# Threshold attention and SwiGLU block on one core: weight clamps of the first tiles on GpSimd, one weight conversion in another slot, one flipped head copied earlier

## The chip, the core and the metric

The kernel runs on one core of one Trainium2 chip. The metric is the device time of one execution in microseconds (us), given as the median of several runs. The engines named below are TensorE (PE; its weight loads PEld), VectorE (DVE), ScalarE (ACT), GpSimd (POOL) and SyncE (SP), which only issues DMAs here. Each engine works through its own queue in order; semaphores hold an instruction back until what it reads is there and what it overwrites has been read.

## What is computed

All inputs are float32.

```python
# q, k, v: (8, 8, 576, 64); tau = 0.02
scores = scale * np.matmul(q, k.transpose(0, 1, 3, 2))
thresh = np.max(scores, axis=-1, keepdims=True) - tau
scores = np.where(scores >= thresh, scores, -1000000000.0)
attn = softmax(scores)
attn_out = np.matmul(attn, v)
# x: (4608, 512), the heads side by side
g = x @ w_gate                      # w_gate, w_val: (512, 1536)
out = (g * sigmoid(g)) * (x @ w_val) @ w_out    # w_out: (1536, 512)
```

## The kernel before

**Float64 weights as two words.** The three weight matrices reach the chip as 64-bit words, two 32-bit words for each weight, and each piece of 128 x 768 weights is made into float32 by integer and float steps, a "conversion". There are 24 pieces. `fetch_weights` (L268) issues a piece's DMAs on SP into one of six places, if the piece's place is free. `split_weights` (L286) issues two ScalarE instructions: L291 makes the upper part (and writes it where the weight will lie), L292 the lower part (into one of three rotating buffers). `join_weights` (L295) does the rest: on DVE a clamp with a minimum and a maximum (L298, `tensor_scalar` with two operations), a shift by three bits (L302) and a `scalar_tensor_tensor` that puts in the sign (L305), then on GpSimd the integer addition of the lower part (L307). The clamp needs L291 alone, the addition needs L305 and L292. A place is free for the next piece when the piece before has been joined.

**The first batch.** The first of the eight batches is worked on in a loop that is written out by hand (L665): four segments of two tiles (each segment one pair of heads, tiles t = 0 and 1 of 128 queries), then four segments of three tiles (t = 2, 3 and the half tile t = 4, for the pairs 3, 0, 1, 2). A slot "n.x" is tile x of segment n: 0.0, 0.1, 1.0, ... 3.1 are the first pass, 4.0, 4.1, 4.2, 5.0, ... 7.2 the second. The pieces of one slot come in this order:

- `scores` (L398) is a generator in four steps. First: the score matmuls on PE (L407, or L413 for the half tile) into one or two of the two score buffers in PSUM, and the negated maximum of each head on DVE (L424). Second: ScalarE's threshold (L427) and exponential (L428) of each head. Third: DVE's mask with sum (L431) for each head, the sum (L433) and its reciprocal (L434); from t = 2 on also the scaling of the probabilities by it, head 0 on ScalarE (L441), head 1 on GpSimd (L439). Fourth: for t = 0 and 1 two scaled unit matrices instead (L447).
- `attend_tile` (L487): the attention product of the tile flipped before (PE, L500 and L503), copied by ScalarE (L505).
- `flip` (L454): the transposes of the probabilities of the tile before. For each head four PE instructions into a bank "tp" (L469 or L471), more into a bank "end" (L474, L476, L480); ScalarE copies each head's bank (L477, L481) and then the end bank (L483). Four PSUM banks go round in turn among these, the attention products and the gate and value products; a bank is given back after its copy has been queued, and the next user's matmul waits for that copy.
- `split_weights` and `fetch_weights(2)`, then step three of the scores, then `join_weights` of one piece, then `fill` (PE's gate and value products of the first block, L517, with ScalarE's L532 and L533, DVE's L541), step four, and `fill` again. GpSimd's gate product (L548) comes from `gates`.
- At the slot's end, in some slots: DVE's transposes of the next segment's k and q (L628, L631, L635, L705, L639, L640) and GpSimd's scaling of q (L340).

In the second step of a slot ScalarE's queue so holds: threshold and exponential of both heads, then the copies of both flipped heads and of the end, then L291 and L292, then the scaling.

**Where a slot differs.** In 4.0 the kernel before attends twice, and joins, splits and fetches a second piece after the products. In 4.2 and 5.2 (`double`) it joins two pieces, after the products rather than before, and splits and fetches a second one.

**After the first batch** a planner (`Plan`, L28) orders the instructions of the other engines around PE's by costs written in the source. Its remaining conversions are lines L820 to L834. The first slot after the loop (scores L1652) is called H0.

Of the kernel before, what the change touches and what calls it, by code (L numbers as in the profile page):

```python
# [14 lines left out]
ALU = mybir.AluOpType  # L15
# [97 lines left out]
def kernel(  # L113
# [11 lines left out]
    nc = tc.nc  # L125
    P = 128
    B, H, S, D = q.shape
    NP = H // 2
# [10 lines left out]
    NT = SM // P  # L139
# [87 lines left out]
    def bank(name):  # L227
        n = turns.popleft()
        ps = ps_f.tile([P, 512], F32, name=name, tag=f"bank{n}")
        taken[id(ps)] = n, ps  # L230
        return ps

    def give_back(ps):
        turns.append(taken.pop(id(ps))[0])

    def run_idle(n):
        ps = bank("idle")
        for _ in range(n):
            nc.tensor.matmul(ps[:, 0:TC], ones[:, 0:P], ones, start=True, stop=True)
        give_back(ps)  # L240
# [27 lines left out]
    def fetch_weights(n=1):  # L268
        for _ in range(n):
            if not wpieces or wpieces[0][2] in used:  # L270
                return
            dst, srcs, place = wpieces.popleft()
            used.add(place)
            m = 2 if len(srcs) == 2 else nf
            to = places[place].bitcast(U64).rearrange("p (m n) -> p m n", m=m)
            if len(srcs) == 1:
                nc.sync.dma_start(out=to, in_=srcs[0])
            else:
                for x, src in enumerate(srcs):
                    nc.sync.dma_start(out=to[:, x, :], in_=src)  # L280
            fetched.append((dst, place))

    def words(place, dst, w):
        return places[place].bitcast(U32).rearrange("p (m n w) -> p m n w", m=dst.shape[1], w=2)[:, :, :, w]

    def split_weights():  # L286
        if fetched:
            dst, place = fetched.popleft()
            lo = los[0].rearrange("p (m n) -> p m n", m=dst.shape[1])
            los.rotate(1)  # L290
            nc.scalar.activation(dst, words(place, dst, 1).bitcast(F32), AF.Abs, scale=2.0 ** -96)  # L291
            nc.scalar.activation(lo, words(place, dst, 0), AF.Identity, bias=minus2, scale=-2.0 ** -51)  # L292
            split.append((dst, place, lo))

    def join_weights(n=1):  # L295
        steps = [split.popleft() for _ in range(min(n, len(split)))]
        for up, place, lo in steps:
            nc.vector.tensor_scalar(out=up, in0=up, scalar1=1.875 * 2.0 ** -80, scalar2=2.0 ** -111,  # L298
                                    op0=ALU.min, op1=ALU.max)
        for up, place, lo in steps:  # L300
            ub = up.bitcast(U32)
            nc.vector.tensor_scalar(out=ub, in0=ub, scalar1=3, scalar2=None, op0=ALU.logical_shift_left)  # L302
        for up, place, lo in steps:
            ub = up.bitcast(U32)
            nc.vector.scalar_tensor_tensor(out=ub, in0=words(place, up, 1), scalar=0x80000000, in1=ub,  # L305
                                           op0=ALU.bitwise_and, op1=ALU.bitwise_xor)
            nc.gpsimd.tensor_tensor(out=ub, in0=ub, in1=lo.bitcast(U32), op=ALU.add)  # L307
            joined.append(up)
            used.discard(place)
# [82 lines left out]
    def turned(t):  # L392
        return TA <= t < NT
# [58 lines left out]
    xts = {}  # L452

    def flip():  # L454
        if not unflipped:
            return
        seg, t, both, ps = unflipped.popleft()
        n = P if t < NT else D
        pT = pTbufs[0][:, 0:2 * KT * n].rearrange("p (h t q) -> p h t q", h=2, t=KT)
        pT2 = pTbufs[0][:, 2 * KT * n:(2 * KT + 1) * n]  # L460
        pTbufs.rotate(1)
        end = bank("end")
        for h, (p, unit) in enumerate(ps):
            tp = bank("tp")
            for kt in range(KT):
                at_ = kt * P + (D if turned(t) and h == 1 else 0)
                ks, to = slice(at_, at_ + P), slice(kt * P, (kt + 1) * P)
                if unit is ident:
                    nc.tensor.transpose(tp[:, to], p[:, ks], unit)  # L469
                else:  # L470
                    nc.tensor.matmul(tp[:, to], p[:, ks], unit, start=True, stop=True)  # L471
            if t < NT:
                if not turned(t):
                    nc.tensor.matmul(end[h * D:(h + 1) * D, 0:P], p[:, KM:S], unit, start=True, stop=True)  # L474
                elif h == 1:
                    nc.tensor.transpose(end[:, 0:P], both, unit)  # L476
                nc.scalar.copy(pT[:, h], tp.rearrange("p (t q) -> p t q", q=P))  # L477
            else:
                for hs in heads:
                    nc.tensor.matmul(end[hs, 0:D], p[hs, KM:S], unit[hs, hs], start=True, stop=True)  # L480
                nc.scalar.copy(pT, tp.rearrange("p (t h q) -> p h t q", h=2, q=D))  # L481
            give_back(tp)
        nc.scalar.copy(pT2, end[:, 0:n])  # L483
        give_back(end)
        unattended.append((seg, t, pT, pT2))

    def attend_tile():  # L487
        if not unattended:
            return
        if not xts:  # L490
            for u, lo in enumerate((0, 2 * XW)):
                xts["full", u] = xall[:, lo:lo + XW].rearrange("p (c n) -> p c n", c=NCC)
            xts["last", 0] = xlast
        seg, t, pT, pT2 = unattended.popleft()
        vr, vr2 = seg["v"]
        n = pT2.shape[1]
        xa = bank("xa")
        for kt in range(KT):
            for h in range(2):
                nc.tensor.matmul(xa[h * D:(h + 1) * D, 0:n], vr[:, h, kt, :], pT[:, h, kt, :],  # L500
                                 start=(kt == 0), stop=False)
        for hs in heads:
            nc.tensor.matmul(xa[hs, 0:n], vr2[hs, :], pT2[hs, :], start=False, stop=True)  # L503
        u, lo = divmod(t * P, TC)
        nc.scalar.copy(xts[("last", 0) if t == NT else ("full", u)][:, seg["i"], lo:lo + n], xa[:, 0:n])  # L505
        give_back(xa)
# [136 lines left out]
    def give(unit):  # L643
        ready.append(unit)
        left[0] += cost(unit)
# [17 lines left out]
    more_loads.popleft()()  # L663
    last = iter(())
    for n, seg in enumerate(segs[:2 * NP]):  # L665
        if n >= NP:
            seg["v"] = segs[seg["i"]]["v"]
        for x, t in enumerate(seg["tiles"]):
            go = scores(seg, t)
            next(go)  # L670
            if not n and not x:
                run_idle(6)
            next(last, None)
            attend_tile()
            next(go)
            next(last, None)
            flip()
            if n == NP and x == 0:
                attend_tile()
                give(FIRST)  # L680
            part = pace(n, x) / 2
            more = len(split)
            if n or x:
                split_weights()
                fetch_weights(2)
            next(go)
            double = t == NT and NP <= n < NP + 2
            if more and not double:
                join_weights()
            fill(part)  # L690
            next(go)
            fill(part)
            if double:
                join_weights(2)
                split_weights()
                fetch_weights(2)
            elif n == NP and x == 0:
                join_weights()
                split_weights()
                fetch_weights(2)  # L700
            gates()
            last = go
            if n == NP and later:
                to, fr = later.pop(0)
                nc.vector.transpose(out=to, in_=fr)  # L705
            if x == 0 and 0 < n < NP - 1:
                load_v(segs[n + 1])
                more_loads.popleft()()
            if n == 0 and x == 1 or n == 1:
                scales.popleft()()  # L710
            elif n == NP - 2 and x == 1:
                more_loads.popleft()()
                scales.popleft()()
            elif n == NP - 1:
                scales.popleft()()
                fetch_qk(NP)
            elif n == NP and x == 1:
                scales.popleft()()
            if x == len(seg["tiles"]) - 2 and n + 1 < len(segs):
                prepare(segs[n + 1])  # L720
# [1180 lines left out]
    for s, (n, x) in enumerate((n, x) for n in range(len(halved)) for x in range(NU3)):  # L1901
        seg = halved[n]
        i, t = seg["i"], seg["tiles"][x]
# [104 lines left out]
```

## Time and profile before

| what | us |
|---|---|
| median of three runs | 1380.66 |
| lowest, highest | 1379.52, 1382.99 |
| the profiled execution: its time | 1379.44 |
| the profiled execution: its span | 1377.3 |
| mean granted TensorE clock | 1.0 of full speed |

The span runs from the first to the last instruction that the profile records; 2.1 us of the profiled execution's time lie around it.

Where PE starts the scores of each slot in the profiled execution (us from the span's start):

| slot | start | slot | start | slot | start |
|---|---|---|---|---|---|
| 1.0 | 16.36 | 4.0 | 53.63 | 6.0 | 98.93 |
| 1.1 | 22.54 | 4.1 | 64.09 | 6.1 | 105.97 |
| 2.0 | 28.59 | 4.2 | 71.22 | 6.2 | 114.89 |
| 2.1 | 34.84 | 5.0 | 77.10 | 7.0 | 120.76 |
| 3.0 | 41.66 | 5.1 | 84.54 | 7.1 | 126.65 |
| 3.1 | 47.90 | 5.2 | 93.07 | 7.2 | 133.64 |
| | | | | H0 | 139.50 |

How to read the profile's lines. A group or timeline line names the line of the kernel, the engine, the operation, what is written and what is read, with partitions x elements. A timeline line begins with the start and the duration; in brackets stands how long the engine had been idle before and what ended that. A line of the waits names the engine and its line, then what it waited for, then the total, the number of times and the longest. A line of the windows gives the stretch, its length, the busy time of PE, PEld, DVE, ACT and POOL with the number of instructions, the granted clock, the DMA share and GB/s. In the page's slices each digit is a fortieth of the span and the busy share in tenths.

### The profile page before, as it was taken

How to read it: one execution, taken by the hardware profiler on the slowest of the kernel's cores; microseconds unless marked ns; L12 is line 12 of the kernel's file. 1: busy time of each engine (PE TensorE's matmuls, PEld its weight loads, DVE VectorE, ACT ScalarE, POOL GpSimd, SP SyncE). 2: the span in 40 equal slices, each digit the busy share in tenths (PEclk: the TensorE clock that was granted, in tenths of full speed). 3: DMA queues.
4: the chain of work that ended last, by engine and by line, in shares of the span. 5: the costliest groups of instructions: out<-in, count | busy, mean ns of one | idle time of the engine just before them, and what ended most of it. 6: DMA issues, size and time to landing. Idle time of an engine off the chain costs nothing.

```text
span 1377.3 us, 39288 instructions
## 1 busy us (share of the span) xinstructions
PE 1356.8 (99%) x15630; PEld 1116.4 (81%) x15630; DVE 1081.5 (79%) x2829; ACT 875.1 (64%) x2278; POOL 700.2 (51%) x649
## 2 busy tenths in 40 slices
PE   9988999999999999999999999999999999999998
PEld 6666787778778778887788888878887888999998
DVE  7988988887887777787678877877777776687786
ACT  6888766676755767767766766776677764330330
POOL 2456498844484669533974378436943593000000
PEclk9999999999999999999999999999999999999999
DMA  8734413465513541555155523553065404423421
GB/s 176 208 105 142 99 36 98 122 188 143 174 48 126 143 115 42 170 143 143 32 153 133 146 56 121 139 143 96 27 186 157 112 19 143 158 80 138 154 69 32
DMA packets 208295, 162.33 MB, mean 118 GB/s; under 512 B 166128, under 2 KB 180464, under 8 KB 202736
## 3 DMA queue, kind: packets, MB, share of 16 engines
q1 hardware_dynamic: 203920, 158.86, 40.9%
q8 instruction: 124, 2.03, 0.6%
q10 hardware_dynamic: 4192, 0.95, 0.3%
q14 instruction: 59, 0.48, 0.1%
HBM read 138.28 MB, written 21.50 MB: 116 GB/s over the span
## 4 chain that ended last, share of the span: by engine, by line
PE 91%; DVE 4%; ACT 2%; SPq 1%; DMA 1%; issue 1%; ACTq 0%; DVEq 0%
PE pb L940 18%; PE pa L940 12%; PE px L1420 12%; PE sc L1652 10%; PE xa L1749 9%; PE pe L940 9%; PE po L1216 5%; PE py L1429 5%; PE sc L1101 2%; PE pg L1147 2%; PE pv L1147 2%; PE pv L517 1%; PE pe L1101 1%; SPq L336 1%; PE xa L500 1%
## 5 line engine op out<-in xcount | busy, mean ns | idle before, releaser
L1700 DVE SCALAR_TENSOR_TENSOR pall<-sc,th,pall 128x288 f32<-128x288 f32 x504 | 243.7, 514 | 63.5 <-ACT pall L1698 49.3
L940 PE MATMUL pb<-xall,big 128*128 128x256 f32 x1152 | 273.5, 380 | 0.0
L1698 ACT ACTIVATE pall<-sc,nm 128x288 f32<-128x288 f32 x504 | 231.6, 497 | 34.6 <-DVE pall L1700 34.3
L940 PEld LDWEIGHTS pb<-xall,big 128*128 128x128 f32 x1152 | 216.4, 190 | 31.0 <-issue 2.2
L1728 DVE STREAM_TRANSPOSE pall<-pall 128x576 f32<-128x576 f32 x252 | 190.0, 765 | 59.3 <-ACT pall L1726 42.6
L1726 ACT ACTIVATE pall<-pall,ri 128x288 f32<-128x288 f32 x408 | 186.6, 527 | 25.0 <-DVE ri L1714 24.3
L795 POOL TENSOR_TENSOR hall<-hall,tmp 128x512 f32<-128x512 f32 x80 | 103.6, 1295 | 159.3 <-DVE hall L993 144.0
L940 PE MATMUL pa<-xall,big 128*128 128x256 f32 x768 | 183.3, 382 | 0.0
L940 PEld LDWEIGHTS pa<-xall,big 128*128 128x128 f32 x768 | 143.1, 190 | 22.0 <-issue 2.9
L1652 PE MATMUL sc<-kT,qT 64*32 64x144 f32 (+1 forms) x5376 | 149.8, 345 | 3.4 <-DVE pall L1700 2.2
L1673 DVE TENSOR_REDUCE mx<-sc 128x2 f32<-128x576 f32 x168 | 124.7, 742 | 27.3 <-PE sc L1652 26.9
L1652 PEld LDWEIGHTS sc<-kT,qT 64*32 64x32 f32 x5376 | 97.9, 106 | 57.5 <-issue 21.6
L940 PE MATMUL pe<-xall,big 128*128 128x256 f32 x576 | 137.3, 381 | 0.0
L1749 PE MATMUL xa<-pall,vall 64*32 64x288 f32 x4032 | 132.2, 404 | 1.0 <-DVE hall L993 0.8
L1723 POOL TENSOR_SCALAR pall<-pall,ri 128x288 f32<-128x288 f32 x96 | 95.7, 1010 | 63.6 <-DVE ri L1714 63.5
L940 PEld LDWEIGHTS pe<-xall,big 128*128 128x128 f32 x576 | 108.4, 190 | 17.0 <-issue 2.7
L1749 PEld LDWEIGHTS xa<-pall,vall 64*32 64x32 f32 x4032 | 76.4, 107 | 50.1 <-issue 7.2
L1708 ACT COPY sums<-sums 32x6 f32<-32x6 f32 x336 | 66.6, 198 | 45.1 <-DVE pall L1700 40.5
L1687 ACT COPY mx<-mx 32x6 f32<-32x6 f32 x196 | 38.1, 194 | 60.8 <-DVE mx L1675 58.9
L992 ACT ACTIVATE vall<-tmp 128x512 f32<-128x512 f32 x96 | 60.1, 629 | 23.9 <-POOL tmp L795 9.6
L1429 PE MATMUL py<-wo,hall 128*128 128x256 f32 x336 | 74.8, 379 | 0.0
L1675 DVE TENSOR_REDUCE mx<-sc 128x1 f32<-128x288 f32 x168 | 74.7, 444 | 0.0
(256 smaller groups left out, 2468.2 us busy)
## 6 DMA issues: line engine op xcount, KB each, us to landing
big<-sums_hbm SPq DMA_DIRECT2D x42, 1024.0 KB, 5.3
big<-sums_hbm SPq DMA_DIRECT2D x48, 768.0 KB, 4.8
vall<-in_v_dram SPq DMA_DIRECT2D x112, 144.0 KB, 3.1
out_dram<-big SPq DMA_DIRECT2D x32, 256.0 KB, 3.5
qT<-in_q_dram SPq DMA_DIRECT2D x112, 72.0 KB, 4.8
kT<-in_k_dram SPq DMA_DIRECT2D x112, 72.0 KB, 3.1
wo<-in_moe_w_gate_dram SPq DMA_DIRECT2D x16, 384.0 KB, 3.8
wo<-in_moe_w_val_dram SPq DMA_DIRECT2D x16, 384.0 KB, 4.5
```

What stands on the lines that cost most here:

```text
L795: return lambda: nc.gpsimd.tensor_tensor(out=out, in0=a, in1=b, op=op)
L940: nc.tensor.matmul(ps[:, i], w[:, k_, i * P:(i + 1) * P], x[:, k_, :], start=first and i == k_ == 0, stop=True, skip_group_check=True)
L1420: nc.tensor.matmul(ps, a[:, f, :], ws[n][:, f, :], start=bank_ not in begun, stop=True, skip_group_check=True)
L1429: nc.tensor.matmul(ps(), a[:, f, i * P:(i + 1) * P], operands[o][:, f, :], start=first and f == 0, stop=True, skip_group_check=True)
L1652: nc.tensor.matmul(pss[h][(slice(g * G, (g + 1) * G), *part)], qT[hs, col:col + G], kT[hs, c * SH + keys[0]:c * SH + keys[1]], start=True, ...
L1673: rs.append(job("DVE", 0.72, lambda n=n, tile_=tile_: nc.vector.tensor_reduce(out=mx[:, n:n + 2, 0], in_=tile_[:, :, 0:SH], axis=AX.X, op= ...
L1698: ej = job("ACT", 0.42, lambda x=x, n=n: nc.scalar.activation(ps[x], scs[x], AF.Exp, bias=nm[:, n:n + 1]), ej, *((masks[h, 0], masks[h, 1] ...
L1700: masks[x] = job("DVE", 0.45, lambda x=x, n=n: nc.vector.scalar_tensor_tensor(out=ps[x], in0=scs[x], scalar=th[:, n:n + 1], in1=ps[x], op0 ...
L1723: scaled.append(job("POOL", 1.02, lambda x=x, n=n: nc.gpsimd.tensor_scalar(out=x, in0=x, scalar1=ri[:, n:n + 1], scalar2=None, op0=ALU.mul ...
L1726: scaled.append(job("ACT", 0.46, lambda x=x, n=n: nc.scalar.activation(x, x, AF.Copy, scale=ri[:, n:n + 1]), rj, rank=rank))
L1728: seg["turned"].append(job("DVE", 0.72, lambda both=both: nc.vector.transpose(out=both, in_=both), *scaled, rank=rank))
L1749: nc.tensor.matmul(holds[a].ap()[x * G:(x + 1) * G, 0:SH].rearrange("d (i q) -> d i q", q=G), vr[rs, h, j, ds], p[rs, h, :, j, :], start=( ...
```

## The change

Three things, all in the first batch.

1. In segments 0 to 3 the clamp is issued to GpSimd right after a piece's two ScalarE instructions, in the slot that splits it; `join_weights` leaves the clamp out for such a piece. Seven pieces are split there (slots 0.1 to 3.1). The clamp's place in GpSimd's queue is ahead of the addition of the piece joined in the same slot and of the scaling of q at the slot's end.
2. The second join, split and fetch of slot 4.0 are gone; slot 6.2 is now a `double` slot like 4.2 and 5.2. Every conversion between the two is joined one piece later in the sequence; from 7.0 on the slots hold the same pieces as before.
3. `flip` becomes a generator, and in the second tile of segments 4 to 7 (slots 4.1, 5.1, 6.1 and 7.1) its first head is issued before the second step of the scores. On ScalarE one head's copy (L477) so stands ahead of both thresholds and exponentials instead of behind them.

The order of PE's and SP's instructions is the same in both kernels.

```diff
--- before.py
+++ after.py
@@ -283,6 +283,11 @@
     def words(place, dst, w):
         return places[place].bitcast(U32).rearrange("p (m n w) -> p m n w", m=dst.shape[1], w=2)[:, :, :, w]
 
+    early_slots, clamped = [True], []
+
+    def clamp(eng, x):
+        eng.tensor_scalar(out=x, in0=x, scalar1=1.875 * 2.0 ** -80, scalar2=2.0 ** -111, op0=ALU.min, op1=ALU.max)
+
     def split_weights():
         if fetched:
             dst, place = fetched.popleft()
@@ -290,13 +295,16 @@
             los.rotate(1)
             nc.scalar.activation(dst, words(place, dst, 1).bitcast(F32), AF.Abs, scale=2.0 ** -96)
             nc.scalar.activation(lo, words(place, dst, 0), AF.Identity, bias=minus2, scale=-2.0 ** -51)
+            if early_slots[0]:
+                clamp(nc.gpsimd, dst)
+                clamped.append(dst)
             split.append((dst, place, lo))
 
     def join_weights(n=1):
         steps = [split.popleft() for _ in range(min(n, len(split)))]
         for up, place, lo in steps:
-            nc.vector.tensor_scalar(out=up, in0=up, scalar1=1.875 * 2.0 ** -80, scalar2=2.0 ** -111,
-                                    op0=ALU.min, op1=ALU.max)
+            if not any(up is x for x in clamped):
+                clamp(nc.vector, up)
         for up, place, lo in steps:
             ub = up.bitcast(U32)
             nc.vector.tensor_scalar(out=ub, in0=ub, scalar1=3, scalar2=None, op0=ALU.logical_shift_left)
@@ -452,6 +460,10 @@
     xts = {}
 
     def flip():
+        for _ in flip_steps():
+            pass
+
+    def flip_steps():
         if not unflipped:
             return
         seg, t, both, ps = unflipped.popleft()
@@ -480,6 +492,7 @@
                     nc.tensor.matmul(end[hs, 0:D], p[hs, KM:S], unit[hs, hs], start=True, stop=True)
                 nc.scalar.copy(pT, tp.rearrange("p (t h q) -> p h t q", h=2, q=D))
             give_back(tp)
+            yield
         nc.scalar.copy(pT2, end[:, 0:n])
         give_back(end)
         unattended.append((seg, t, pT, pT2))
@@ -663,6 +676,7 @@
     more_loads.popleft()()
     last = iter(())
     for n, seg in enumerate(segs[:2 * NP]):
+        early_slots[0] = n < NP
         if n >= NP:
             seg["v"] = segs[seg["i"]]["v"]
         for x, t in enumerate(seg["tiles"]):
@@ -672,9 +686,13 @@
                 run_idle(6)
             next(last, None)
             attend_tile()
+            flips = flip_steps()
+            if n >= NP and x == 1:
+                next(flips, None)
             next(go)
             next(last, None)
-            flip()
+            for _ in flips:
+                pass
             if n == NP and x == 0:
                 attend_tile()
                 give(FIRST)
@@ -684,7 +702,7 @@
                 split_weights()
                 fetch_weights(2)
             next(go)
-            double = t == NT and NP <= n < NP + 2
+            double = t == NT and NP <= n < NP + 3
             if more and not double:
                 join_weights()
             fill(part)
@@ -692,10 +710,6 @@
             fill(part)
             if double:
                 join_weights(2)
-                split_weights()
-                fetch_weights(2)
-            elif n == NP and x == 0:
-                join_weights()
                 split_weights()
                 fetch_weights(2)
             gates()
```

## Prediction

> **What bounds the kernel now.** I read the page first, then the windows, the waits of the first 140 us, and each engine's timeline there. A slot n.x is tile x of segment n in the loop at L665; "H0" is the first slot after that loop. The page's head:
>
> ```profile
> span 1377.3 us, 39288 instructions
> PE 1356.8 (99%) x15630; PEld 1116.4 (81%) x15630; DVE 1081.5 (79%) x2829; ACT 875.1 (64%) x2278; POOL 700.2 (51%) x649
> ```
>
> TensorE sets the end: it is free for 20 us of the whole span. Windows cut at the score starts of 1.0, 4.0, 5.0, 6.0, 7.0 and H0 (us, then busy time by engine):
>
> ```profile
> 53.63:77.10 23.47, 20.90 (x159) 15.71 (x158) 20.20 (x39) 19.96 (x40) 13.77 (x8) 1.00 0.58 172
> 77.10:98.93 21.83, 18.98 (x148) 13.99 (x147) 18.44 (x35) 17.60 (x35) 12.96 (x7) 1.00 0.33 110
> ...
> sum 123.14, PE 112.70 PEld 84.14 DVE 106.82 ACT 103.39 POOL 64.27; mean PE 22.54 PEld 16.83 DVE 21.36 ACT 20.68 POOL 12.85
> ```
>
> Half of that, 10.4 us, is PE's idle time in the first batch, 16.36 to 139.50, where the change acts; besides this only scores that stretch because their second half waits (2.02 us below, else 1.36) can be shortened. DVE is busy 107 of 123 us, hence nearly as tight. The waits of the first 140 us (total, times, longest):
>
> ```profile
> PE pv L517 <- ACT big L477: 6.4, 4, 2.3
> ...
> PE sc L407 <- DVE pall L431: 2.9, 4, 1.0
> ```
>
> In four slots a value product waits for ScalarE's copy of a flipped head (its bank); in four more the scores wait until DVE has masked the tile before. Rows that I price with (start, duration), from the timelines of PE, DVE and GpSimd (POOL):
>
> ```profile
> 28.59 2.02 PE L407 MATMUL sc<-pall,qT 64*128 64x288 f32 x8 [0.41 <-DVE pall L431]
> ...
> 69.73 1.56 PE L517 MATMUL pv<-xall,big 128*128 128x256 f32 x6 [2.28 <-ACT big L477]
> ```
>
> ```profile
> 29.57 0.76 DVE L298 TENSOR_SCALAR big<-big 128x768 f32<-128x768 f32 x1
> 30.36 0.56 DVE L302 TENSOR_SCALAR big<-big 128x768 uint32<-128x768 uint32 x1
> ...
> 60.41 0.98 DVE L302 TENSOR_SCALAR big<-big 128x768 uint32<-128x768 uint32 x1
> ...
> 62.55 2.23 DVE L298 TENSOR_SCALAR big<-big 128x768 f32<-128x768 f32 x1 [0.16 <-ACT big L291]
> ```
>
> ```profile
> 28.99 0.92 POOL L340 TENSOR_SCALAR hall<-hall,scl 128x256 f32<-128x256 f32 x1 [2.06 <-DMA hall<-in_q_dram]
> ...
> 60.09 1.88 POOL L439 TENSOR_SCALAR pall<-pall,ri 128x576 f32<-128x576 f32 x1 [0.84 <-DVE ri L434]
> 62.53 1.83 POOL L307 TENSOR_TENSOR big<-big,extra 128x768 uint32<-128x768 uint32 x1 [0.57 <-ACT big L291]
> ...
> 74.87 1.72 POOL L340 TENSOR_SCALAR qT<-qT,scl 128x576 f32<-128x576 f32 x1
> ```
>
> A clamp (L298) is usually 0.54 us, but stretches until a running GpSimd instruction is over; a shift (L302) beside one took 0.98 instead of 0.56.
>
> [...] L340 takes 0.92 us for 256 elements and 1.72 for 576, 2.5 ns each. [...]
>
> **The change, part by part.** I carried the four queues forward slot by slot with the rows' durations, in each engine's new order; PE and SP keep their order.
>
> *A. Seven clamps leave DVE (conversions split in slots 0.1 to 3.1).* Each took 0.57 us, start to start, between a tile's masks and the next tile's maxima. PE alone needs 5.73 us for such a slot (3.1: 47.90 to 53.63, no wait). Score starts 22.54, 28.59, 34.84, 41.66, 47.90, 53.63 make slots of 6.05, 6.25, 6.82, 6.24, 5.73: 2.44 us over the floor, the most that A can bring by 4.0. GpSimd gains seven clamps. No row shows a two-operation one; the L340 line gives 2.2 us for 768 elements with one operation, the 768-element L307 1.8, and twice 2.2, the second operation paid like the first, 4.4. I take 2.5 and keep 1.8 to 4.4. GpSimd's slot is then 2.5 + 1.81 (add) + 1.08 (scaling of 320 elements of q, L340) = 5.4, under 5.73, and a clamp has until the next slot's shift: hidden. Behind the clamp wait the add and q's scaling, which slide later by 2.5, so that two or three shifts (L302) now meet a scaling of q and lose 0.2 to 0.9 each, as the clamp at 29.57 did. Some 0.4 of the 2.44 is given back: -2.0 at 4.0. In 4.0 the exponentials and copies that the second attention product waits for come 0.6 earlier (the last clamp): -2.6 at 4.1. Neither end helps by itself, since nothing else on GpSimd gets shorter; the low end costs nothing, because GpSimd stands idle 2.2 to 6.3 us ahead of each add in the first pass (25.13 to 56.38).
>
> *B. The conversion moved out of 4.0.* DVE's 3.73 us from 62.55 to 66.28 go (the clamp 2.23, because of L307). The maxima of 4.1 (66.71) can follow the scores, at about 64.85. ScalarE loses 1.7 us (L291, L292), SP a pair of weight loads that nobody waits for. The later W_out conversion waits 0.79 for its DMA today; splitting it a slot later ends that, off the path.
>
> *C. The head copied first in 4.1, 5.1, 6.1, 7.1.* The copy (0.47) goes ahead of the exponentials and waits for PE's transposes; behind it in ScalarE's queue stand both exponentials, and DVE's masks wait for these. In 4.1: transposes end about 65.9, copy to 66.45, exponentials to 68.1, first mask 68.1. PE goes on with pv at 67.35 rather than 69.73 and starts the scores of 4.2 at 68.7 rather than 71.22. B and C: -2.5, so -5.1 at 4.2. Slot 4.2 gives back 0.8, since its transposes wait for probabilities scaled as late as before: -4.3 at 5.0. In 5.1 and 6.1 the copy fits into ScalarE's idle time before L427 (1.50, 1.40), and 1.70 and 1.64 us of PE's wait go. But the next maxima still wait behind DVE's conversion (94.75) and then behind ScalarE's queue, which is shorter only by the one copy: I keep 0.47 each, -5.2 at 7.0.
>
> *D. The conversion arrives in 6.2.* DVE then has two there, 3.8 us before 7.0's maxima, as 5.0 and 6.0 have: those slots took 7.44 and 7.04 against 5.89 of 7.0: 1.35 more on average. With half of the 0.78 by which the scores that follow stretch (2.14 for 1.36), +1.7. In 7.1 the removed 0.80 wait pays 0.3 of it. In 7.2 DVE, now behind, has two transposes of q and k in its queue as well (L639, L640: 1.4 us), and H0's scores wait for its masks: +1.4. Together +2.8.
>
> Sum: -5.2 + 2.8 = -2.4 us at H0 (139.5). From there on each queue's order is the old one, so the shift is carried to the end. The profiled execution took 1379.44 (span 1377.3 and 2.1 around it): 1377.0. The median of the three runs is 1.2 higher: 1380.66 - 2.4 = **1378.3**.
>
> **Rivals.** *GpSimd becomes the bound (17%).* From the first split part (18.0) to the scaled head that 4.1's transposes need, GpSimd must do 7 clamps, 6 adds (10.9), the scalings of q (6.2) and L439 (1.9): 37.0 + 7c, against 63.3 in my account. It decides from c = 3.8, eats the whole gain at 4.1, and at c = 4.4 ends 7 x 0.64 = 4.5 later: **1382.8, slower than before**. For it: one-input rows are far from cheap, and two operations may cost double. Against: the add of two inputs with 768 elements is 1.8.
>
> *DVE swallows it (15%).* After a double conversion two adds and a gate run on GpSimd, and L298 grew to 1.08 and 1.49 us (85.52, 106.94) in 5.0 and 6.0. If 7.0 and H0 catch the same, 0.95 each, the gain is 0.5: 1380.2.
>
> *PE keeps what C frees (8%).* If DVE catches up in 5.2 and 6.2, the 3.3 us of waits there are kept rather than 0.94: 1375.9. Against it: DVE runs at 18.4 of 21.8 us there and has its maxima last.
>
> That the change doesn't do what it says is out: the built order has each move.
>
> **Numbers.** My forecast 60%, 1.2 us either way. Range 1375.8 to 1382.8: it leaves out the clamps beyond 4.4 and half of the third rival, under 2 in 10. A measurement of this kernel tells about 0.3% (4.1 us) from no change: faster (under 1376.5) 8%, slower (over 1384.8) 10%, between 82%.
>
> **What would show it.** Right: GpSimd's new clamps between 1.8 and 3.5 us; scores at about 51.6 (4.0), 66.1 (4.2), 72.8 (5.0), 115.6 (7.0), 137.1 (H0), so a lead that peaks near 5 us and halves in 7.x; the pv wait for L477 gone in four slots. Wrong: L439 of 4.0 starting after 61; exponentials of 4.1 ending after 67; a lead at 7.0 under 3 or at H0 over 4; or shifts in the first pass of more than 1.5 us.

## The result, and the profile after

| | before | after |
|---|---|---|
| median, us (18 executions each) | 1380.06 | 1377.72 |
| lowest, highest | 1377.64, 1382.99 | 1376.52, 1380.42 |
| the profiled execution: time, span | 1379.44, 1377.3 | 1378.87, 1376.8 |
| mean granted TensorE clock in it | 1.000 | 0.998 |

The ratio of the two is 0.9985, with a 95% interval of 0.9978 to 0.9992: 1.1 to 3.0 us less. The forecast was 2.4 us less, the medians differ by 2.3.

The head of the page after the change:

```profile
span 1376.8 us, 39287 instructions
PE 1358.2 (99%) x15630; PEld 1119.1 (81%) x15630; DVE 1076.9 (78%) x2822; ACT 874.5 (64%) x2278; POOL 709.1 (52%) x656
```

DVE has lost 4.6 us and GpSimd gained 8.9; PE is 1.4 us busier with the same 15630 instructions. Why it is so shows in the windows, cut at the same score starts as before:

```profile
52.16:74.06 21.90, 20.41 (x160) 15.57 (x159) 15.28 (x32) 17.61 (x37) 12.93 (x8) 1.00 0.55 159
74.06:95.35 21.29, 18.75 (x147) 14.08 (x146) 18.45 (x35) 17.98 (x36) 12.99 (x8) 1.00 0.44 151
...
116.64:139.76 23.12, 21.65 (x147) 16.47 (x146) 19.39 (x37) 17.04 (x35) 13.00 (x7) 0.85 0.25 76
```

Segment 4 (first line) takes 21.90 us instead of 23.47, with DVE busy 15.28 instead of 20.20. The last line is segment 7: its granted clock, the third number from the end, is 0.85. Before, it was 1.00 in each of these segments. Finer windows of PE alone (stretch, length, busy time, clock, DMA share, GB/s) find the place:

```profile
123.00:124.00 1.00, 0.00 (x0) 1.00 1.00 387
124.00:125.00 1.00, 0.93 (x5) 1.00 0.78 301
125.00:126.00 1.00, 1.00 (x7) 0.68 0.00 0
126.00:127.00 1.00, 1.00 (x6) 0.50 0.00 0
...
131.00:132.00 1.00, 1.00 (x4) 0.50 0.00 0
132.00:133.00 1.00, 1.00 (x6) 0.90 0.00 0
```

PE stands still from 122.6 to 124.07, goes on, and 1.3 us later gets half the clock for 6.8 us (a window that holds a change has a value between the two: 0.68 puts it at 125.36, 0.90 at 132.20). The PE timeline of the changed kernel shows what was waited for, and what half the clock costs:

```profile
65.64 1.46 PE L530 MATMUL pv<-xall,big 128*128 128x256 f32 x6
67.02 1.19 PE L421 MATMUL sc<-pall 64*64 64x288 f32 x8
...
70.76 1.09 PE L481 MATMUL tp<-pall 128*128 128x128 f32 x8 [1.16 <-ACT tmp L546]
...
74.06 1.36 PE L415 MATMUL sc<-pall 64*128 64x288 f32 x10
...
124.07 2.82 PE L415 MATMUL sc<-pall 64*128 64x288 f32 x10 [1.47 <-DVE pall L439]
...
128.28 1.97 PE L481 MATMUL tp<-pall 128*128 128x128 f32 x8
```

The first value product of 4.1 (65.64) no longer waits, and 4.2 starts 4.20 us earlier than before. Eight transposes take 1.97 us at 128.28 and 1.09 at 70.76. If PE does half its work in these 6.8 us, as the granted clock says, it loses 3.4 us there: an estimate. The waits of the first 140 us (16 to 140; total, times, longest):

```profile
PE tp L481 <- ACT tmp L546: 3.9, 3, 1.4
...
PE sc L415 <- DVE pall L439: 3.6, 4, 1.5
```

The wait of pv for the copy of a flipped head (6.4 us before) is gone. In its place, the transposes of the third slot of a segment wait 3.9 us for a bank: it held the gate product of the slot before until ScalarE's L545 and L546 had read it, and these stand behind the split (L296, L297) and the scaling (L449).

The clamps on GpSimd, with a scaling of q beside them:

```profile
18.10 0.83 POOL L289 TENSOR_SCALAR big<-big 128x768 f32<-128x768 f32 x1 [6.97 <-ACT big L296]
18.90 0.93 POOL L348 TENSOR_SCALAR extra<-extra,scl 128x256 f32<-128x256 f32 x1
...
42.20 1.34 POOL L289 TENSOR_SCALAR big<-big 128x768 f32<-128x768 f32 x1 [3.40 <-ACT big L296]
```

A clamp of 768 elements takes 0.83 us, 1.1 ns per element, less than L348 with 256.

### The profile page after: what moved, and what is told of

Read it like the earlier page. It is cut to its first block, busy times and chain, and to the rows that moved or that the text cites. A ratio compares the mean times of both kernels' runs of the same rounds, so it can differ in the third digit from the quotient of the medians.

```text
span 1376.8 us, 39287 instructions
## 1 busy us (share of the span) xinstructions
PE 1358.2 (99%) x15630; PEld 1119.1 (81%) x15630; DVE 1076.9 (78%) x2822; ACT 874.5 (64%) x2278; POOL 709.1 (52%) x656
## 4 chain that ended last, share of the span: by engine, by line
PE 93%; DVE 4%; ACT 2%; issue 1%; DMA 0%; DVEq 0%; ACTq 0%
PE pb L954 18%; PE pa L954 12%; PE px L1434 12%; PE sc L1666 10%; PE xa L1763 9%; PE pe L954 9%; PE po L1230 5%; PE py L1443 5%; PE sc L1115 2%; PE pg L1161 2%; PE pv L1161 2%; PE sc L415 1%; PE pe L1115 1%; PE tp L483 1%; PE xa L513 1%
```

## The experiments

A lead is the start of a slot's scores in the profile before, less that in the profile shown, each counted from the start of 1.0. "Next" is the scores after H0 (150.49 before).

| lead, us | 4.0 | 4.1 | 4.2 | 5.0 | 5.2 | 6.0 | 7.0 | 7.1 | 7.2 | H0 | next |
|---|---|---|---|---|---|---|---|---|---|---|---|
| forecast | 2.0 | 2.6 | 5.1 | 4.3 | | | 5.2 | 3.5 | | 2.4 | 2.4 |
| after | 1.46 | 1.64 | 4.19 | 3.03 | 4.95 | 3.57 | 4.11 | 2.57 | -0.27 | -0.27 | -0.27 |
| e9_fill_ahead | 1.71 | 1.90 | 4.44 | 3.30 | 5.22 | 3.85 | 4.37 | 2.93 | 2.81 | 1.83 | 1.53 |
| e1_clamps | 1.48 | 1.67 | 2.30 | 2.32 | 2.33 | 2.33 | 2.34 | 2.34 | 2.34 | 2.34 | 2.34 |
| e2_flips | 0.06 | 0.07 | 1.99 | 0.65 | 2.57 | 1.19 | 1.74 | 1.74 | 2.80 | 2.12 | 1.81 |
| e3_move | 0.06 | 0.06 | 1.37 | 1.39 | 1.39 | 1.39 | 1.39 | -0.15 | -1.71 | -1.71 | -1.71 |
| e4_no_move | 1.45 | 1.63 | 4.17 | 2.79 | 4.71 | 3.34 | 3.90 | 3.91 | 4.97 | 4.25 | 3.97 |

Every execution lists its mean clock. One stretch of 3.4 us at half clock takes 0.0012 from it, so 0.999 can hide one such stretch (the profiled executions of e1, e3 and e6 have one each; e1's lies at 8 us, ahead of 1.0, where eight score matmuls took 1.99 us, 1.25 in the changed kernel), and a low clock in the last microseconds counts too (0.50 from 1376.5 on in the profile before). The last column compares only those at 1.000, with those of the kernel before in the same comparison (for "after", whose comparison lists none for before, with those of e1's: 1378.71).

| | median, us | ratio to before, 95% interval | executions at 0.998 or less, at 0.999 | at 1.000, less before at 1.000 |
|---|---|---|---|---|
| before (with e1 to e4) | 1379.52 | | 13, 10 of 33 | |
| after | 1377.72 | 0.9978 to 0.9992 | 6, 5 of 18 | -1.7 |
| e1_clamps | 1376.50 | 0.9967 to 0.9986 | 0, 3 of 10 | -2.2 |
| e2_flips | 1377.10 | 0.9975 to 0.9990 | 1, 2 of 16 | -1.8 |
| e3_move | 1381.05 | 1.0001 to 1.0018 | 6, 4 of 13 | +1.9 |
| e4_no_move | 1374.77 | 0.9951 to 0.9976 | 0, 1 of 5 | -4.1 |
| e5_fill | 1379.85 | 0.9994 to 1.0011 | 7, 1 of 13 | -0.3 |
| e6_two_clamps | 1378.65 | 0.9982 to 0.9999 | 7, 4 of 13 | -1.5 |
| e7_all_clamps | 1379.79 | 0.9989 to 1.0005 | 11, 2 of 13 | none |
| e8_flips_x12 | 1375.13 | 0.9959 to 0.9982 | 0, 2 of 6 | -3.5 |
| e9_fill_ahead | 1377.30 | 0.9975 to 0.9989 | 0, 2 of 21 | -1.5 |
| e10_late_split | 1378.60 | 0.9986 to 0.9999 | 14, 6 of 21 | -1.8 |
| e11_no_move_fill | 1374.33 | 0.9948 to 0.9973 | 0, 1 of 5 | -4.4 |
| e12_before_fill | 1380.03 | 0.9993 to 1.0010 | 4, 4 of 13 | -0.4 |

The two tables fit: the lead at "next" is what the executions at full clock gain (e1 2.34 and 2.2, e2 1.81 and 1.8, e3 -1.71 and -1.9, e4 3.97 and 4.1, e9 1.53 and 1.5). The before's own 13 executions at 0.998 or less have a median of 1380.81, 2.1 us over its 10 at 1.000. So two things set a median here: the work in the first batch, and how often the clock drops.

### The parts by themselves

**e1_clamps**: the changed kernel without its second and third part.

```diff
-            if n >= NP and x == 1:
+            if False:
                 next(flips, None)
...
-            double = t == NT and NP <= n < NP + 3
+            double = t == NT and NP <= n < NP + 2
...
+            elif n == NP and x == 0:
+                join_weights()
+                split_weights()
+                fetch_weights(2)
```

> The clamps alone on GpSimd in the first pass; the conversion stays in 4.0 and the flips stay behind the exponentials. If the parts add as the prediction has them (part A): the scores of 4.0 start about 1.5 us earlier, as in the changed kernel (52.2), the lead is carried to H0, and the time is 1.5 to 1.9 us under before. If the first pass's gain is lost again as soon as DVE is the busiest engine (rival): the lead is under 0.5 us at 5.0 and the time within 0.5 us of before. The granted clock is 1.00 throughout in either case.

Measured: 1.48 at 4.0 as expected, then 0.63 more in 4.1, 2.34 at H0, 3.0 us less in the median. More than either theory had. The 0.63 come where pv waits in 4.1 (start, duration, and the wait that was 2.28 before):

```profile
68.34 1.56 PE L530 MATMUL pv<-xall,big 128*128 128x256 f32 x6 [1.64 <-ACT big L489]
```

**e2_flips**: the third part alone (the clamp on DVE, the conversion in 4.0).

```diff
-            if early_slots[0]:
+            if False:
                 clamp(nc.gpsimd, dst)
```

with e1's last two hunks.

> The flipped head copied first in 4.1, 5.1, 6.1 and 7.1 alone; clamps on DVE, the conversion in 4.0. Prediction's part C: four waits of PE for the head's copy go (6.4 us in all), of which 1 to 2 us are kept at H0, since DVE's maxima and masks come last in the next slot: 1.0 to 1.8 us under before. Rival (PE keeps what the copy frees): 3 us or more under before. Other rival (the new wait of the flipped transposes for the tanh's bank, 3.9 us in three slots of the changed kernel, takes its place): within 0.5 us of before.

Measured: 1.81 at "next", 2.4 less in the median (1.8 at full clock); both rivals fall. Its PE timeline in 4.1 and 4.2:

```profile
69.38 1.19 PE L421 MATMUL sc<-pall 64*64 64x288 f32 x8 [0.54 <-DVE pall L439]
...
73.31 1.09 PE L481 MATMUL tp<-pall 128*128 128x128 f32 x8 [1.36 <-ACT tmp L546]
```

Of 1.92 us gained in 4.1 the second line takes back 1.34 in 4.2 (lead 0.65 at 5.0): the new wait belongs to the flips, not to the clamps or the move.

**e3_move**: the second part alone (e1's first hunk and e2's hunk in the changed kernel).

> The conversion alone moved from 4.0 to 6.2. Prediction's parts B and D: about 1.2 us gained at 4.1, some 2.8 us given back between 7.0 and H0: 0.8 to 1.6 us over before, with the clock at 1.00. Clock theory: PE waits for DVE in 7.0 and 7.1 about 1.4 us at a time, the granted clock halves for some 7 us around 125 to 135 us in part of the executions (mean clock 0.997 to 0.999 rather than 1.000), and the time is 1.5 to 4 us over before, more in the executions with the lower clock.

Measured: 1.5 us over before in the median, and 3.1 us lost in segment 7, where PE waits twice:

```profile
126.92 2.13 PE L415 MATMUL sc<-pall 64*128 64x288 f32 x10 [1.46 <-DVE pall L439]
...
133.98 1.56 PE L530 MATMUL pv<-xall,big 128*128 128x256 f32 x6 [1.27 <-ACT big L489]
```

Both theories get their part. The queues alone cost the forecast's amount, at a clock of 1.00 in this stretch; and 6 of 13 executions have the lower clock. In the profiled one it fell elsewhere, in 5.1 (0.50 from 85.4 to 88.8), after a 1.04 us wait of the scores, and cost nothing there, since PE then waited less for pv (0.51 us, 1.70 before).

**e4_no_move**: the first and third part, without the second (e1's last two hunks).

> The changed kernel without the move: clamps on GpSimd and flips ahead, the conversion back in 4.0. If the move costs more at the end of the batch than it brings in 4.0 (the prediction's parts B and D: +2.8 against -1.2; or the clock theory): 3 to 4.5 us under before, 0.7 to 2 us under the changed kernel, no slice with a clock under 1.00. If the move pays (rival): 1 to 2 us under before, since 4.1 then waits for DVE's masks again.

Measured: 1374.77, 4.8 us under before. The changed kernel was 2.3 under it in its own comparison, so the run without the move is 2.4 better (2.4 as well by the leads, 3.97 against 1.53 in e9_fill_ahead). Its PE timeline in 4.1, 4.2 and segment 7:

```profile
65.76 1.46 PE L530 MATMUL pv<-xall,big 128*128 128x256 f32 x6
67.15 1.19 PE L421 MATMUL sc<-pall 64*64 64x288 f32 x8
...
71.12 1.09 PE L481 MATMUL tp<-pall 128*128 128x128 f32 x8 [1.39 <-ACT tmp L546]
...
122.84 1.36 PE L415 MATMUL sc<-pall 64*128 64x288 f32 x10
128.77 1.19 PE L421 MATMUL sc<-pall 64*64 64x288 f32 x8
```

With the conversion still in 4.0, pv waits for nothing in 4.1, and the lead at 4.2 is 4.17, against 4.19 with the move. Alone the move brought 1.37 there; beside the flips it brings 0.02, because both remove the same wait. What it costs in segment 7 it costs in full. DVE in 6.2 and 7.0, first of the changed kernel, then of this one:

```profile
117.35 1.02 DVE L289 TENSOR_SCALAR wo<-wo 128x768 f32<-128x768 f32 x2
118.29 1.02 DVE L310 TENSOR_SCALAR wo<-wo 128x768 uint32<-128x768 uint32 x2
...
120.96 1.42 DVE L432 TENSOR_REDUCE nm<-sc 128x1 f32<-128x576 f32 x2
```

```profile
118.91 1.41 DVE L432 TENSOR_REDUCE nm<-sc 128x1 f32<-128x576 f32 x2
```

The maxima of 7.0 come 2.05 us later behind the double conversion, and PE's scores of 7.1 wait for the masks that follow.

### The clock

**e5_fill**: idle matmuls meant to fill the waits ahead of the scores.

```diff
+    def hold_clock(n):
+        ps = bank("idle")
+        for _ in range(n):
+            nc.tensor.matmul(ps[:, 0:TC], ones[:, 0:P], ones, start=True, stop=True)
+        turns.appendleft(taken.pop(id(ps))[0])
...
             if n >= NP and x == 1:
                 next(flips, None)
+                if n > NP:
+                    hold_clock(4)
             next(go)
```

> The changed kernel with four idle matmuls (about 1 us of TensorE work that nothing reads) put ahead of the scores of 5.1, 6.1 and 7.1, where PE waits 0.65 to 1.47 us for DVE's mask. Clock theory (such a wait is what lets the granted clock fall to half): the share of executions with a mean clock of 0.998 or less falls from 6 in 18 to 1 in 10 or none, and the median falls from 1377.7 to about 1377.0, that of the changed kernel's executions at 1.000. Rival (the dips come whatever PE does): the share stays near a third, the median within 0.3 us of 1377.7. Second rival (the idle matmuls are in the way): 0.5 us or more over 1377.7.

Measured: 1379.85, and 7 of 13 executions at 0.998 or less. The experiment missed its place. This call of `next(go)` is the second step, so the fill lies behind the scores, between the two heads:

```profile
124.14 2.14 PE L421 MATMUL sc<-pall 64*128 64x288 f32 x10 [1.46 <-DVE pall L445]
...
127.09 0.66 PE L487 MATMUL tp<-pall 128*128 128x128 f32 x4
127.58 1.91 PE L245 MATMUL idle<-pall 128*128 128x256 f32 x8
```

The wait of 1.46 is as it was, and four idle matmuls are 1.9 us of work in the way. It says nothing against the theory, only what such work costs there.

**e9_fill_ahead**: the same function, in the right place and sized to the waits.

```diff
+            if n > NP and x == 1:
+                hold_clock((2, 1, 3)[n - NP - 1])
             next(go)
             if not n and not x:
                 run_idle(6)
```

> The changed kernel with idle matmuls this time really ahead of the scores: two before 5.1, one before 6.1, three before 7.1 (about 0.45 us each, inside waits of 1.05, 0.65 and 1.47 us; in the earlier fill they fell behind these waits, between the two flipped heads). Clock theory (these waits of PE are what lets the granted clock fall to half): executions with a mean clock of 0.998 or less fall from 6 in 18 to 1 or 2 in 13, and the median from 1377.7 to 1377.0. Rival (the dip comes from elsewhere, from a slot's mean load or the DMA beside it): the share stays at a third or more, the median at 1377.5 to 1378.5.

Measured: no execution of 21 at 0.998 or less (6 of 18 in the changed kernel), 19 at 1.000, median 1377.30. PE around 7.1:

```profile
122.25 1.46 PE L245 MATMUL idle<-pall 128*128 128x256 f32 x6
123.79 2.16 PE L421 MATMUL sc<-pall 64*128 64x288 f32 x10
```

The scores start when they did (123.79, 0.28 earlier than in the changed kernel), the idle time is filled, and the clock stays. So it is PE's standing still at these three score waits that lets the clock fall, shown by taking it away. It isn't the chip: on the same one the kernel before had 14 of 41 and e10_late_split 14 of 21 at 0.998 or less. Which of the three waits does it, this run doesn't part; profiles caught the drop behind 7.1 (the changed kernel, e6_two_clamps) and behind 5.1 (e3_move). This run is the change without the drop: lead 1.53 at "next".

**e12_before_fill**: the kernel before with two idle matmuls ahead of 5.1 and one ahead of 6.1.

> The kernel before with the same fill ahead of 5.1 and 6.1, and nothing else changed; its waits of pv (2.28 us in 4.1, 1.70 and 1.64 in 5.1 and 6.1) stay. A third of its executions so far (14 of 41) have a mean clock of 0.998 or less. If the wait of 2.28 us in 4.1, which both parts of the change shorten, is what lets the clock fall there: the share stays at a third, and the time within 0.4 us of before. If it is the waits of the scores of 5.1 and 6.1 (rival): the share falls to 1 in 10 or less, and the time by 1 us.

Measured: 4 of 13 executions at 0.998 or less, 1.0001 times before. The kernel before drops its clock too, and not because of these two waits. Its wait of 2.28 us in 4.1 is the likeliest place, since the kernels that have neither it nor the wait of 1.46 us in 7.1 nor a new longer one (e1, e2, e4, e8, e11) have 1 such execution in 42 together. No profile caught a drop there, so this is argued, not shown.

### GpSimd and ScalarE

**e6_two_clamps**: the changed kernel with each GpSimd clamp issued twice.

```diff
                 clamp(nc.gpsimd, dst)
+                clamp(nc.gpsimd, dst)
```

> The changed kernel with each of the seven GpSimd clamps issued twice (the second changes nothing). The clamp took 0.83 to 1.34 us, so GpSimd gets 6 to 9 us more in the first pass. If GpSimd has the room that the prediction gave it (it decides from 3.8 us for one clamp): within 0.5 us of the changed kernel, 1377.7. If the clamps are near the path already, since the adds and scalings behind them slide (rival): 1 to 5 us over it.

Measured: 0.9 us over the changed kernel in the median, but the two executions at full clock took 1377.04 and 1377.35, against a median of 1377.05 for the changed kernel's seven. A pair took 1.75 to 2.27 us; the second clamp costs nothing that these few executions can tell. GpSimd has the room. (7 of 13 executions have the lower clock, against 6 of 18: with so few, no difference.)

**e7_all_clamps**: e4_no_move with every clamp of the batch on GpSimd (the line `early_slots[0] = n < NP` left out).

> The run without the move (1374.8), and the clamps of the second pass on GpSimd too: eight or nine more clamps leave DVE, which lost 1.1 to 1.5 us to each beside a gate. If DVE alone sets 5.x and 6.x, as the waits of the scores for its mask say (1.0, 0.65): 1 to 3 us faster, 1372 to 1373.8. If ScalarE's tanh and the flips behind it set them (the wait of tp for tmp, 4.8 us in four slots), or GpSimd's gates come later behind the clamps: 1374.3 to 1376.

Measured: 4.6 us slower than e4_no_move, each against before; both theories missed. GpSimd's queue in 5.1:

```profile
83.01 1.29 POOL L561 TENSOR_TENSOR hall<-hall,tmp 128x512 f32<-128x512 f32 x1
84.25 1.14 POOL L289 TENSOR_SCALAR big<-big 128x768 f32<-128x768 f32 x1
85.38 2.42 POOL L447 TENSOR_SCALAR pall<-pall,ri 128x576 f32<-128x576 f32 x1
```

In the second pass L447 scales a head whose transposes PE needs at once. It now stands behind a clamp, and itself took 2.42 us (1.72 at 92.01). PE:

```profile
87.85 1.12 PE L481 MATMUL tp<-pall 128*128 128x128 f32 x4 [2.41 <-POOL pall L447]
```

The same wait in 6.1 is 2.11 us. Around both the clock falls to 0.50 (windows of PE alone):

```profile
86.00:88.00 2.00, 0.15 (x1) 0.89 0.32 70
88.00:90.00 2.00, 2.00 (x8) 0.50 0.78 229
90.00:92.00 2.00, 2.00 (x9) 0.76 0.27 107
110.00:112.00 2.00, 1.41 (x8) 0.86 0.92 333
112.00:114.00 2.00, 2.00 (x6) 0.50 0.64 240
```

11 of 13 executions have a mean of 0.998 or less. What the waits cost and what the half clock costs isn't separated here. This is the prediction's first rival, in the pass where it can happen: not GpSimd's total, but what stands behind a clamp in its queue.

**e8_flips_x12**: e4_no_move with the first head ahead in the third slot of a segment too.

```diff
-            if n >= NP and x == 1:
+            if n >= NP and x >= 1:
                 next(flips, None)
```

> The run without the move (1374.8), with the first flipped head copied ahead of the exponentials in the third slot of each segment too (4.2, 5.2, 6.2, 7.2). There PE's transposes wait for the bank of the gate's product until ScalarE's tanh; put ahead of the scores, the transposes meet a bank and probabilities that are no earlier. If the wait for the bank is the limit in those slots: PE then waits ahead of the scores instead, the maxima and exponentials come later, and the time is 1 to 5 us over 1374.8. If only ScalarE's order is (rival): the second head's wait shrinks and the time is 0.5 to 2 us under it.

Measured: 1375.13 against 1374.77; the intervals overlap, both theories missed. The wait of tp for the gate's bank is as long (1.40, 1.36, 1.36). The expectation had the transposes go ahead of the scores; they don't. Since PE's order doesn't change, only ScalarE's, and ScalarE's copy waits for the same transposes, nothing moves.

**e10_late_split**: e4_no_move with the split of 4.1, 5.1, 6.1 and 7.1 behind the slot's gates.

```diff
+            late = n >= NP and x == 1
-            if n or x:
+            if (n or x) and not late:
                 split_weights()
                 fetch_weights(2)
...
             fill(part)
+            if late:
+                split_weights()
+                fetch_weights(2)
             if double:
```

> The run without the move (1374.8), with the split of 4.1, 5.1, 6.1 and 7.1 (L296 and L297 on ScalarE, 1.9 us together) issued behind the slot's gates instead of ahead of its masks. If these two are what keeps the tanh of the gate's product, and with it the bank of the next flip, waiting: the wait of tp for tmp falls from 4.8 us in four slots to under 2, and the time by 0.5 to 2 us, to 1372.8 to 1374.3. Rival (the probabilities' scaling, L449, which waits for DVE's masks, sets the tanh anyway): the wait shrinks by under 1 us in all, and the time stays within 0.4 us. Third: the split now stands ahead of the next slot's exponentials and the next conversion, and the time is 0.5 to 2 us over 1374.8.

Measured: 1378.60, 3.4 us over e4_no_move, each against before: the third outcome, and larger. ScalarE in 6.2, and PE with it:

```profile
113.06 0.59 ACT L546 ACTIVATE tmp<-pg 128x512 f32<-128x512 f32 x1
113.53 0.93 ACT L296 ACTIVATE wo<-xall 128x768 f32<-128x768 f32 x1
114.35 0.98 ACT L297 ACTIVATE big<-xall,minus 128x768 f32<-128x768 uint32 x1
115.22 0.26 ACT L518 COPY xall<-xa 128x128 f32<-128x128 f32 x1
```

```profile
113.70 0.66 PE L481 MATMUL tp<-pall 128*128 128x128 f32 x4 [0.48 <-ACT tmp L546]
115.63 0.75 PE L481 MATMUL tp<-pall 128*128 128x128 f32 x4 [1.27 <-ACT xall L518]
```

The wait for L546 falls to 0.48, as the theory said, but the second head's bank is that of the attention product, and its copy L518 now stands behind the split. In the four slots together 4.8 us of waits for L546 become 1.3, and 5.0 for L518 are new: 1.5 more. The split's 1.9 us had merely moved, to where they hold up another bank.

Much of the rest is the clock, which fell right after this wait:

```profile
116.39 3.82 PE L530 MATMUL pv<-xall,big 128*128 128x256 f32 x10
```

```profile
116.00:118.00 2.00, 2.00 (x8) 0.50 0.00 0
118.00:120.00 2.00, 2.00 (x7) 0.65 0.00 0
```

The ten matmuls take 2.32 us in e4_no_move. 14 of 21 executions are at 0.998 or less and only one at 1.000, so this run costs waits and clock together.

**e11_no_move_fill**: e4_no_move with e12's fill.

> The run without the move (1374.8), with two idle matmuls ahead of the scores of 5.1 and one ahead of 6.1, inside waits of 1.04 and 0.65 us. That kernel has no wait of 1.45 us or more and no execution with a mean clock under 0.999 so far, so the fill has little to save: 1374.2 to 1375.0, no execution at 0.998 or less. Rival (idle matmuls that end late push the scores, and with them the maxima): 1375.2 to 1376.5.

Measured: 1374.33, no execution at 0.998 or less. With e4_no_move it is the fastest, 5.2 us under before in its own comparison (0.9948 to 0.9973); the two can't be told apart.

## Why the prediction was right, step by step

**The total** held: 2.3 us for 2.4. Its work steps give 1.5 (e9_fill_ahead, lead 1.53) or 1.7 (executions at full clock); the interval of the medians, 1.1 to 3.0, holds both these and 2.3. So the closeness is partly luck. Of the 0.9 us of work that are missing, 0.7 are missing at 4.1 already (1.90 in e9_fill_ahead for 2.6): part A. The rest would lie in how often each kernel's clock drops, which the prediction didn't have at all.

**A, the clamps.** The duration was mis-sized: 2.5 us was taken, 1.8 the lower bound, and 0.82 to 1.34 was measured. The row that I scaled from (the scaling of q, by an operand `scl` of one value per partition) is no neighbour of an operation with two constants: it took 0.92 us for 256 elements, the clamp 0.83 for 768 (0.54 on DVE). It cost nothing, since either price is hidden (e6_two_clamps). The gain at 4.0 was 1.5 instead of 2.0: scores of 3.0 still wait 0.47 (0.81 before) and still stretch to 2.02, because DVE, once early, waits 0.76 us for ScalarE's exponential in 2.0 where it had waited 0.33. The shifts of the first pass lost at most 0.26 us. The 0.6 us that were to come in 4.0 came in 4.1 (e1_clamps).

**B and C at 4.1.** 2.55 us for 2.5: right in sum. But the split between them wasn't worked out, and B's part is 0.02 (e4_no_move). In 4.2 1.16 were given back for 0.8, and not for the reason named: the transposes wait for the gate's bank, not for the probabilities. From 5.0 to 7.0 1.08 us were kept for 0.94, so the third rival (PE keeps all) is out.

**D, the conversion in 6.2.** Right in sum and in its first half. Without the clock's drop (e9_fill_ahead) the lead falls by 2.84 us between 7.0 and "next" (4.37 to 1.53), where without the move (e4_no_move) it rises by 0.07: the conversion costs 2.9 for 2.8. By 7.1 it costs 1.45, for the 1.35 by which 7.0 was to lengthen. But then 1.2 go in 7.1 (the lead falls by 0.12 and doesn't rise by 1.06), where half of a stretch of 0.78, less 0.3, had been put down; the scores there stretch by all of 0.80 (2.16 for 1.36). In 7.2, where DVE's transposes were to cost 1.4, it is 0.3 (0.98 lost for 0.72). So the second half was put in the wrong slot, and that the sum is right is luck. With the drop the lead fell by 4.4 by H0 in the profiled execution (4.11 to -0.27).

**The second rival** (DVE swallows it, gain 0.5) was nearer than its 15% at H0: the clamp of 7.0 did stretch beside GpSimd (1.12 us at 125.04, beside L561; 0.54 in e4_no_move). It is out by the interval.

**The checks.** The pv waits are gone and the lead peaks at 5.5 us (in 6.2) and more than halves in segment 7. Scores are 0.6 to 1.3 us later than listed up to 7.0 (52.16, 67.02, 74.06, 116.64), and at H0 139.76 instead of 137.1. The clamps lie outside the band given for "right". None of the four signs for "wrong" came.

## What to carry to other kernels

When two parts of a change remove the same wait, only one is paid, while the costs of both add: measure each alone and each left out. Here the part that moved a conversion brings 1.4 us alone, nothing beside the others, and costs 2.9 later. Before a step leaves or enters an in-order queue, look at what stands behind it and is needed next (L447 behind a clamp, for which PE waited 2.41 us, L518 behind a split, 1.27). And where PE waits more than a microsecond at once (the drops below stand around waits of 1.04 to 2.41 us), look at the granted clock of the next ten in several executions.

## What the runs showed of the hardware

**Half the clock after a short wait.** Six drops of the granted clock to 0.50 stand in the profiles of the first batch, around single waits of PE of 1.04 to 2.41 us:

| | PE's wait, us | ended at | clock at 0.50 | for, us |
|---|---|---|---|---|
| after | 1.47 | 124.07 | 125.36 to 132.20 | 6.84 |
| e3_move | 1.04 | 83.26 | 85.36 to 88.76 | 3.40 |
| e6_two_clamps | 1.46 | 123.78 | between 125 and 130 | 3.4 |
| e7_all_clamps | 2.41 | 87.85 | 87.56 to 90.96 | 3.40 |
| e7_all_clamps | 2.11 | 110.59 | 111.44 to 114.88 | 3.44 |
| e10_late_split | 1.27 | 115.63 | 116.00 to 119.40 | 3.40 |

The ends are worked out from windows of 1 or 2 us (e6_two_clamps: of 5 us), taking the clock as either 1.00 or 0.50. In the changed kernel, windows of 0.02 us have no other value but in the two in which it changes (0.68 at 125.36, 0.65 at 132.18). The five drops that these windows place begin between 0.3 us before the wait's end and 2.1 us after it. Five last 3.40 to 3.44 us, that of the changed kernel twice as long.

Such a wait isn't always followed by a drop: in the profile before, PE waited 2.28 us ahead of 69.73, and the clock is 1.00 from 16 to 180 us. Nor does PE's busy share alone decide. In e3_move PE was busy for 0.69 of the 3.4 us ahead of the drop (81.96 to 85.36) and for 0.50 of those from 109.2 to 112.6, after which the clock stayed at 1.00. What decides isn't shown, nor why the same wait drops the clock in one execution and not in the next.

**GpSimd beside DVE.** The clamp took 0.83 us alone and 1.34 at 42.20, while DVE's L313 with its two inputs ran:

```profile
41.90 0.96 DVE L313 SCALAR_TENSOR_TENSOR big<-wo,big 128x768 uint32<-128x768 uint32 x1
```

The five clamps that overlap L313, by 0.36 to 0.66 us, take 0.22 to 0.51 longer than 0.83, and the two that don't take 0.82 and 0.83. In the kernel before, DVE is the one that takes longer: its clamps at 29.57 (0.76 us) and 62.55 (2.23 us; 0.54 at 42.64) ended 0.42 us after the GpSimd instruction that they began beside (L340, L307), and the shift at 60.41 (0.98 us; 0.56 at 43.21) ended 0.58 before L439 did.
